# An attention kernel in fp32: another order of eight matmuls in 60 of 1024 steps, and four weight casts a layer given from ScalarE to GpSimd

## The chip, the cores and the metric

The kernel runs on one core of a Trainium2 chip. The metric is the device time of one execution in microseconds (us); lower is better. Times of several executions are given by their median. A profile is one execution recorded instruction by instruction; its times are counted from the first instruction of the program.

Engines are named as in the profile: PE is TensorE (its weight loads are listed apart, as PEld), DVE is VectorE, ACT is ScalarE, POOL is GpSimd, SP is SyncE, which issues most DMAs.

## The reference

Two kinds of layer alternate, twice each, on x of 2048 tokens by 512 values, all in fp32:

```python
x = x + fourier(layernorm(x))     # y = Cr @ (xn @ Dr.T) - Ci @ (xn @ Di.T)
x = x + attention(layernorm(x))   # 32 query heads of 16 values, one shared key and value head
```

The attention is where the change lies:

```python
q = (x @ wq).reshape(B, S, 32, 16).transpose(0, 2, 1, 3)
k, v = x @ wk, x @ wv
p = softmax(einsum("bhqd,bkd->bhqk", q, k) * 16 ** -0.5)
o = einsum("bhqk,bkd->bhqd", p, v).transpose(0, 2, 1, 3).reshape(B, S, 512) @ wo
```

## The kernel before, in words

A "layer" in the code is one Fourier layer (phase a) and the attention layer behind it (phase b); there are two. Most products are made to fp32 accuracy from numbers in two parts: the high part is the number cast to the fast matmul type `F32R`, the low part is the rest, and three matmuls (high x high, high x low, low x high) make one product (`mm3`, lines 87 to 90).

Phase b (line 1278) goes through 16 blocks of 128 queries. A block has 32 steps: two halves of the heads by 16 tiles of 128 keys. A step n belongs to block `i` and has number `s_` in it. In a step TensorE does, in the order written:

- `pv` (line 1103): for the step two before, the product of the probabilities with the values, 8 matmuls of 128 x 512 into a tile of their own, named z (line 1110).
- In steps 1 and 17 of blocks 1 to 15, `o_proj_part` (line 1179): one half of the previous block's output product with `wo`, 6 matmuls (lines 88 to 90) into a PSUM bank of the group y. ScalarE copies the bank out (line 1185), GpSimd adds it to x (line 1188).
- `score` (lines 1087 to 1099), four times: one matmul of 64 rows by 512 columns into a bank of the group x, and on ScalarE the exponential of it into SBUF (line 1098). Even numbers use rows 0 to 63 of the array, odd numbers rows 64 to 127. A score can run beside a matmul in the other half of the rows.
- Maxima for later blocks. The softmax subtracts row maxima, which are found ahead, from the same scores computed once more: `whole(g)` is one matmul of 512 columns in rows half g (line 436) with a reduction on VectorE (line 437). `part(at, 0)` and `part(at, 1)` fill the two halves of one bank with 256 columns each (line 1056), with a copy of one element on VectorE between them (line 1058) and one reduction over both (line 1061).

`share(n)` says how many maxima a step does. It is three in nearly all steps, and then, if `part_next()` finds work, the order is the string in line 1299, `asMssMsb`: a is `part(at, 0)`, b is `part(at, 1)`, M is `whole`, s is `score`; the digits beside the string are the row half, or for s the number of the score. Otherwise the branch at line 1307 goes score by score. The last steps of the last block have no maxima left.

The maxima and the output product share three PSUM banks, the list `o.banks`. Each use takes the first bank of the list and, when its reader is queued, puts it at the end. So in a usual step a takes the bank of the previous step's first M, the first M that of its second M, and the second M that of its b. In a step that begins with a part of the output product, that product takes the first bank, a and the first M the other two, and the second M takes the output product's bank. Every engine works off its queue in the order written, so a matmul that waits for a bank holds up all behind it on TensorE.

The weights `wo` are loaded in four chunks in steps 12 to 15 of block 0 (line 1317) and split into `woh` and `wol` in steps 20, 22, 24 and 26 (lines 1320 to 1322): ScalarE casts the high part (line 79), GpSimd subtracts it (line 80). GpSimd also prepares the maxima for a coming block (lines 589 and 590, called in steps 9 and 25) and issues half of the small DMAs that put them in place (line 601).

Of the kernel before, what the change touches and what calls it, by code (L numbers as in the profile page):

```python
# [22 lines left out]
NT = S // P  # L23
# [25 lines left out]
def fnet_mqa_kernel(ctx: ExitStack, tc: tile.TileContext, x_in, ct, dt_, wq, wkv, wo, out):  # L49
    nc = tc.nc  # L50
# [5 lines left out]
    def f(ap):  # L56
        return ap.bitcast(F32)

    def slot(k, dtype=F32):
        return sb.tile([P, S], dtype, name=f"slot{k}")  # L60

    def half(k, dtype=F32):
        return sb.tile([P, D], dtype, name=f"row{k}")

    def bank(tag):
        return ps.tile([P, 512], F32, name=tag, bufs={"x": 4, "y": 3, "z": 1}[tag])

    def pair():
        return [bank("x") for _ in range(2)]
# [8 lines left out]
    def split_sb(raw, hi, lo, eng=None):  # L78
        nc.scalar.copy(hi, raw)  # L79
        (eng or nc.vector).tensor_sub(lo, raw, f(hi))  # L80
# [116 lines left out]
    def make_layer(L, src, mid, dst, last):  # L197
# [3 lines left out]
        st = {}  # L201
# [818 lines left out]
        def whole(g):  # L1020
            u = next((u for u in ahead if g in u[3]), None)
            if u is None:
                if not todo or todo[0][0] not in o.loaded | {0}:
                    return
                u = (*todo.pop(0), {0, 1})
                ahead.append(u)
            i, pr, kb, gs = u
            max_half(i, pr, g, kb)
            if i + 1 < NT:
                partial(i + 1)  # L1030
            gs.remove(g)
            if not gs:
                ahead.remove(u)
# [4 lines left out]
        def more_max():  # L1038
            whole(side())

        def part_next():
            if parts:
                return *parts.pop(), 1
            for e, (i, pr, kb) in enumerate(todo):
                if i in o.loaded | {0} and kb > 1:
                    parts.append(todo.pop(e))
                    return *parts[0], 0
            return None
# [28 lines left out]
        def share(n):  # L1077
            slack = min([3 * (at - n) - left(j, lim) for j, lim, at in goals if at > n], default=99)
            st["light"] = slack >= SPARE and not st.get("light") and n >= 4
            return 2 if st["light"] else 3  # L1080
# [6 lines left out]
        def score(i, s_, j):  # L1087
            hf, c = divmod(s_, NT)
            jj, g = divmod(j, 2)
            cp = 4 * (2 * hf + jj)  # L1090
            if (i, s_) not in ptiles:
                k = i * NSTEP + s_
                ptiles[i, s_] = slot((6, 7, 2)[k % 3]).rearrange("p (j n) -> p j n", j=4)
            row = o.banks if i == NT - 1 and jj == 1 and not todo + parts + ahead else o.x
            e = row.pop(0)
            nc.tensor.matmul(e, kz[64 * g:64 * g + KR, c * P:(c + 1) * P],  # L1096
                             o.qT[i][64 * g:64 * g + KR, cp:cp + 4, :], start=True, stop=True)
            nc.scalar.activation(ptiles[i, s_][:, j, :], e, AF.Exp, scale=DH ** -0.5)  # L1098
            row.append(e)
# [3 lines left out]
        def pv(i, s_):  # L1103
            hf, c = divmod(s_, NT)
            if c == 0:
                acc[i, hf] = bank("z")
            a = acc[i, hf]
            pt = ptiles.pop((i, s_))
            for j in range(4):
                nc.tensor.matmul(a[32 * j:32 * j + 32, :], v1[:, c, :], pt[:, j, :], start=c == 0, stop=c == NT - 1)  # L1110
            if c == NT - 1:
                oa = half(hf)
                if last and (i, hf) == (NT - 1, 1):
                    ob = half(0)[:, :256]
                    nc.scalar.copy(oa[:, :256], a[:, :256])
                    nc.vector.tensor_copy(ob, a[:, 256:])
                    oa = (oa, ob)
                else:
                    nc.scalar.copy(oa, a)
                acc[i, hf] = oa  # L1120
# [58 lines left out]
        def o_proj_part(i, hf):  # L1179
            po = o.banks.pop(0)  # L1180
            for k in (2 * hf, 2 * hf + 1):
                ks = slice(k * P, (k + 1) * P)
                mm3(po, bt["oh"][:, ks], bt["ol"][:, ks], woh[:, k, :], wol[:, k, :], k == 2 * hf, k == 2 * hf + 1)
            raw = half(4)
            nc.scalar.copy(raw, po)  # L1185
            o.banks.append(po)
            x = bt["x", i]
            nc.gpsimd.tensor_add(x, raw, x)  # L1188
            if hf:
                (nc.sync if last else nc.gpsimd).dma_start(dst[i], x)  # L1190
# [87 lines left out]
        def phase_b(nxt):  # L1278
            nonlocal woh, wol, osp
            o.x = pair() + pair()  # L1280
            o.banks = [bank("y") for _ in range(3)]
            woh = slot(4, F32R).rearrange("p (k e) -> p k e", k=NK)
            wol = slot(5, F32R).rearrange("p (k e) -> p k e", k=NK)
            def wo_load(j):
                st["wo", j] = half(4 + j)
                nc.sync.dma_start(st["wo", j], wo[:, j, :])

            behind = []
            for n in range(NT * NSTEP):
                i, s_ = divmod(n, NSTEP)  # L1290
                if len(behind) == 2:
                    pv(*behind.pop(0))
                behind.append((i, s_))
                if i > 0 and s_ in (1, NT + 1):
                    o_proj_part(i - 1, s_ // NT)
                n_max = share(n) if todo or parts or ahead else 0
                at = part_next() if n_max == 3 else None
                if at:
                    for k, v in zip("asMssMsb", (0, 1, 0, 3, 0, 1, 2, 1)):
                        if k == "s":  # L1300
                            score(i, s_, v)
                        elif k == "M":
                            whole(v)
                        else:
                            part(at, v)
                else:
                    g = side()
                    for j, m in ((g, 0), (1 - g, min(n_max, 2)), (2 + g, 0), (3 - g, n_max - 2)):
                        score(i, s_, j)
                        for _ in range(m):  # L1310
                            more_max()
                if n in (1, 3):
                    q_half_store(12, 2 + n // 2)
                if i == 0 and 17 <= s_ <= 23 and s_ % 2:
                    q_half_store(14, s_ // 2 - 8)
                if 12 <= n < 16:
                    wo_load(n - 12)
                if n == 25:
                    osp = slot(3, F32R).rearrange("p (a h n) -> p a h n", a=2, h=2)
                if i == 0 and s_ in (20, 22, 24, 26):  # L1320
                    j = s_ // 2 - 10
                    split_sb(st["wo", j], woh[:, j, :], wol[:, j, :], nc.gpsimd)
                if i > 0:
                    for fn in out_tasks(i - 1).get(s_, ()):
                        fn()
                for j in range(2, NT):
                    if i == (j // 4 if j < 5 else j - 4 if j < 13 else j - 2):
                        at = {2: 0, 3: 12, 4: 6}.get(j, 0)
                        if s_ == at:
                            qT_load(j)  # L1330
                        if s_ == at + 4:
                            o.loaded.add(j)
                for fn in half_tasks(i).get(s_, ()):
                    fn()
                for at, j, p0, np_ in ((NT - AHEAD, i, HALF, HALF), (NSTEP - AHEAD, i + 1, 0, HALF if i >= NT - 3 else NPAIR)):
                    if j in (0, NT - 2, NT - 1) or j == i + 1 < NT:
                        for e in range(2):
                            if s_ == at - 1 + e:
                                assert done_with(j, p0 + np_ // 2 * (e + 1) - 1)
                                max_neg_a(j, p0, np_, parts=(e,))  # L1340
                        if s_ == at + 1:
                            max_neg_b(np_, nc.gpsimd)
                        if s_ == at + 2:
                            max_rows(j, p0, np_)
            if nxt is not None:
                nxt.a_start()
            for at in behind:
                pv(*at)
            if nxt is not None:
                o.banks = []  # L1350
            return {**out_tasks(NT - 1), 12: [lambda: o_proj(NT - 1)]}
# [18 lines left out]
        woh = wol = osp = None  # L1370
# [48 lines left out]
```

## Time and profile before

| | us |
|---|---|
| median of 3 runs | 3465.91 (3465.49 to 3466.19) |
| profiled execution | 3465.34 |
| its span, from the first to the last instruction | 3463.6 |
| phase b of the first layer, first to last `pv` | 624.7 to 1733.7 |
| phase b of the second layer, first to last `pv` | 2345.0 to 3452.9 |

The two phases b are 1109 + 1108 us of the span, 64%. The mean granted TensorE clock is 0.999 of full speed.

In the lines of the profile, `L1098 ACT ACTIVATE slot<-x` is an instruction of line 1098 on ScalarE that writes a tile named slot and reads one named x; shapes are partitions by elements. A line of the timeline begins with the start and the duration in us; xN says that N instructions in succession are shown as one; a bracket gives the idle time of the engine before it and what ended it. A line of the waits has who waited, for whom, the sum in us, how often, and the longest. A weight load is issued by TensorE just ahead of its matmul; where the matmul has to wait for a bank or for data, it is the load that stands.

### The profile page before, as it was taken

To read this page: it belongs to the slowest core of one execution; us is meant where nothing else is said; L and a number is where in the kernel's file an instruction comes from. 1 tells how busy PE (TensorE), PEld (TensorE's weight loads), DVE (VectorE), ACT (ScalarE), POOL (GpSimd) and SP (SyncE) were. 2 spreads that over 40 slices of the span, in tenths; PEclk is the share of its full clock that TensorE was granted. 3 is DMA by queue.
4 is the path that set the end of the run, shared out by engine and by line. 5 is a ranking of instruction groups with operands and counts; after the bars stand their busy time and mean duration, and the time that the engine had idled before them with its cause. 6 is when DMAs were issued, how large, how long until landed. Compare 5 with 4: busy or idle time off the path is not lost.

```text
span 3463.6 us, 68751 instructions
## 1 busy us (share of the span) xinstructions
PE 3436.3 (99%) x25536; PEld 2020.8 (58%) x25536; DVE 2661.4 (77%) x5774; ACT 2702.7 (78%) x5384; POOL 971.0 (28%) x1500
## 2 busy tenths in 40 slices
PE   8999999999999999999999999999999999999999
PEld 6887979444444444444378989884444444444443
DVE  6264766899999999999432747668999999999992
ACT  4234644899999999999932256549999999999998
POOL 4255453222232222222313454522111111111111
PEclk9999999999999999999999999999999999999999
DMA  5445252311111101111143352523111111011110
GB/s 188 151 154 189 78 170 81 96 51 32 39 41 47 35 27 26 48 35 27 41 140 116 129 169 100 153 71 90 48 39 36 51 35 38 23 39 36 36 26 26
DMA packets 225556, 255.89 MB, mean 74 GB/s; under 512 B 52896, under 2 KB 175040, under 8 KB 218052
## 3 DMA queue, kind: packets, MB, share of 16 engines
q1 hardware_dynamic: 210932, 234.04, 21.9%
q0 software_dynamic: 14144, 17.33, 1.6%
q8 instruction: 201, 3.29, 0.4%
q14 instruction: 135, 1.11, 0.1%
q10 hardware_dynamic: 144, 0.13, 0.0%
HBM read 187.69 MB, written 65.79 MB: 73 GB/s over the span
## 4 chain that ended last, share of the span: by engine, by line
PE 92%; issue 3%; POOL 2%; ACT 1%; DVE 1%; DMA 1%; SPq 0%; DVEq 0%; ACTq 0%; POOLq 0%
PE z L1110 30%; PE x L1096 13%; PE x L879 11%; PE y L1056 10%; PE y L436 8%; PE y L88 3%; PE y L527 3%; PE y L89 3%; PE y L90 3%; PE x L88 2%; PE x L90 2%; PE x L89 2%; PE z L527 1%; PE y L1096 1%; PE z L275 1%
## 5 line engine op out<-in xcount | busy, mean ns | idle before, releaser
L1098 ACT ACTIVATE slot<-x 128x512 f32<-128x512 f32 x3992 | 2055.9, 610 | 29.7 <-PE x L1096 11.1
L437 DVE TENSOR_REDUCE mxp<-y 128x1 f32<-128x512 f32 x1952 | 1261.0, 686 | 61.6 <-PE y L436 7.1
L1110 PE MATMUL z<-slot,v 128*32 128x512 f32 x8192 | 1095.5, 605 | 0.0
L1096 PE MATMUL x<-slot,kz 64*128 64x512 f32 x2968 | 824.2, 429 | 0.3 <-DMA slot<-craw 0.2
L1061 DVE TENSOR_REDUCE mxp<-y 128x2 f32<-128x512 f32 x960 | 655.1, 682 | 0.9 <-PE y L1056 0.9
L1056 PEld LDWEIGHTS y<-kz,slot 64*128 64x128 f32 x1408 | 258.4, 184 | 571.5 <-DVE mxp L437 554.2
L436 PE MATMUL y<-kz,slot 64*128 64x512 f32 x1440 | 572.3, 418 | 0.7 <-DVE mxp L437 0.4
L1096 PEld LDWEIGHTS x<-slot,kz 64*128 64x128 f32 x2968 | 435.2, 184 | 62.2 <-issue 41.0
L1056 PE MATMUL y<-kz,slot 64*128 64x256 f32 x1408 | 465.8, 331 | 0.3
L879 PE MATMUL x<-cl,xnh 64*128 64x512 f32 (+1 forms) x1536 | 357.2, 353 | 0.0
L879 PE MATMUL x<-ch,xnl 64*128 64x512 f32 (+1 forms) x1536 | 345.0, 358 | 3.4 <-ACT xnl L638 3.4
L879 PE MATMUL x<-ch,xnh 64*128 64x512 f32 (+1 forms) x1536 | 346.1, 358 | 0.2
L436 PEld LDWEIGHTS y<-kz,slot 64*128 64x128 f32 x1440 | 263.4, 185 | 83.6 <-DVE y L1058 23.0
L1110 PEld LDWEIGHTS z<-slot,v 128*32 128x32 f32 x8192 | 164.1, 108 | 221.4 <-issue 182.6
L1188 POOL TENSOR_TENSOR row<-row,row 128x512 f32<-128x512 f32 x60 | 77.0, 1283 | 605.6 <-ACT row L1185 605.2
L879 PEld LDWEIGHTS x<-ch,xnh 64*128 64x128 f32 x1536 | 215.3, 184 | 16.5 <-issue 5.1
L879 PEld LDWEIGHTS x<-ch,xnl 64*128 64x128 f32 x1536 | 213.3, 184 | 19.2 <-issue 6.1
L1058 DVE COPY y<-y 1x1 f32<-1x1 f32 x960 | 141.7, 148 | 104.3 <-PE y L1056 95.3
L879 PEld LDWEIGHTS x<-cl,xnh 64*128 64x128 f32 x1536 | 216.8, 185 | 8.0
L79 ACT CAST ch<-craw 128x512 fp32r<-128x512 f32 x176 | 106.6, 625 | 123.1 <-PE x L90 82.6
L527 PE MATMUL y<-kz,slot 64*128 64x512 f32 x488 | 189.1, 397 | 2.8 <-DVE mxe L543 2.2
L1156 POOL TENSOR_TENSOR row<-row,row 128x256 f32<-128x256 f32 x63 | 46.6, 739 | 483.2 <-DMA row<-rd 467.5
(232 smaller groups left out, 5578.9 us busy)
## 6 DMA issues: line engine op xcount, KB each, us to landing
craw<-ct_in SPq DMA_DIRECT2D x112, 512.0 KB
slot<-qd SPq DMA_DIRECT2D x44, 1024.0 KB
qd<-row SPq DMA_DIRECT2D x144, 128.0 KB
od<-row SPq DMA_DIRECT2D x252, 64.0 KB
row<-wqd SPq DMA_DIRECT2D x48, 256.0 KB
row<-x_in SPq DMA_DIRECT2D x32, 256.0 KB
mid<-row POOLq DMA_DIRECT2D x32, 256.0 KB, 2.4
craw<-ct_in SPq DMA_DIRECT2D x32, 256.0 KB
```

What stands on the lines that cost most here:

```text
L88: nc.tensor.matmul(ps_, ah, bh, start=start, stop=False)
L89: nc.tensor.matmul(ps_, ah, bl, start=False, stop=False)
L90: nc.tensor.matmul(ps_, al, bh, start=False, stop=stop)
L436: nc.tensor.matmul(pm, o.qT[i][gs, pr, :], kz[gs, c0:c0 + n], start=True, stop=True)
L437: nc.vector.reduce_max(to, pm, axis=AX.X)
L527: nc.tensor.matmul(pm, o.qT[i][gs, pr, :], k[gs, c0:c0 + 512], start=True, stop=True)
L879: nc.tensor.matmul(z[d], a[gs, s, d * P:(d + 1) * P], b[gs, :], start=first and q < 2 and e == 0, stop=last and q > 1 and e == len(turns) - 1)
L1056: nc.tensor.matmul(pm[:, 256 * g:256 * g + 256], o.qT[i][gs, pr, :], kz[gs, c0:c0 + 256], start=True, stop=True)
L1061: nc.vector.reduce_max(partial(i)[:, pr, :, k], pm.rearrange("p (a n) -> p a n", a=2), axis=AX.X)
L1096: nc.tensor.matmul(e, kz[64 * g:64 * g + KR, c * P:(c + 1) * P], o.qT[i][64 * g:64 * g + KR, cp:cp + 4, :], start=True, stop=True)
L1098: nc.scalar.activation(ptiles[i, s_][:, j, :], e, AF.Exp, scale=DH ** -0.5)
L1110: nc.tensor.matmul(a[32 * j:32 * j + 32, :], v1[:, c, :], pt[:, j, :], start=c == 0, stop=c == NT - 1)
```

## The change

In steps that begin with a part of the output product, and do a part of the maxima (`at`), the order of the eight matmuls becomes `assssMMb`: all four scores first, then the two whole maxima, that of rows half 1 ahead of that of half 0. The halves still alternate from one matmul to the next. All other steps keep their order.

The split of `wo` moves from steps 20, 22, 24, 26 to steps 16, 18, 20, 22 of block 0, and the cast to the high part is an instruction of GpSimd instead of ScalarE. The subtraction stays on GpSimd.

```diff
-                if i > 0 and s_ in (1, NT + 1):
+                out_now = i > 0 and s_ in (1, NT + 1)
+                if out_now:
                     o_proj_part(i - 1, s_ // NT)
                 n_max = share(n) if todo or parts or ahead else 0
                 at = part_next() if n_max == 3 else None
                 if at:
-                    for k, v in zip("asMssMsb", (0, 1, 0, 3, 0, 1, 2, 1)):
+                    order = zip("asMssMsb", (0, 1, 0, 3, 0, 1, 2, 1))
+                    if out_now:
+                        order = zip("assssMMb", (0, 1, 0, 3, 2, 1, 0, 1))
+                    for k, v in order:
...
-                if i == 0 and s_ in (20, 22, 24, 26):
-                    j = s_ // 2 - 10
-                    split_sb(st["wo", j], woh[:, j, :], wol[:, j, :], nc.gpsimd)
+                if i == 0 and s_ in (16, 18, 20, 22):
+                    j = s_ // 2 - 8
+                    nc.gpsimd.tensor_copy(woh[:, j, :], st["wo", j])
+                    nc.gpsimd.tensor_sub(wol[:, j, :], st["wo", j], f(woh[:, j, :]))
```

## Prediction

> **What bounds the kernel now.** I read the page first: busy shares, then the chain of work that ended last.
>
> ```profile
> PE 3436.3 (99%) x25536; PEld 2020.8 (58%) x25536; DVE 2661.4 (77%) x5774; ACT 2702.7 (78%) x5384; POOL 971.0 (28%) x1500
> ...
> PE 92%; issue 3%; POOL 2%; ACT 1%; DVE 1%; DMA 1%; SPq 0%; DVEq 0%; ACTq 0%; POOLq 0%
> PE z L1110 30%; PE x L1096 13%; PE x L879 11%; PE y L1056 10%; PE y L436 8%; PE y L88 3%; PE y L527 3%; PE y L89 3%; PE y L90 3%; PE x L88 2%; PE x L90 2%; PE x L89 2%; PE z L527 1%; PE y L1096 1%; PE z L275 1%
> ```
>
> TensorE is on the chain nearly everywhere, and the attention steps (L1110 values, L1096 scores, L1056 and L436 maxima) are most of it. An average hides which wait ends last, so I went to the busy times of one stretch: 16 steps of block 4 of the second layer, from one step that begins with a part of the output product (I call it an out step) to the next.
>
> ```profile
> 2515.56:2550.42 34.86, 34.86 (x264) 15.60 (x263) 32.30 (x69) 33.72 (x68) 7.77 (x16) 1.00 0.15 39
> ```
>
> The columns are TensorE, weight loads, VectorE, ScalarE, GpSimd, then the clock. Out of 34.86 us TensorE is busy throughout, ScalarE 33.72 and VectorE 32.30. Three engines are nearly full; whoever gains 0.1 us will meet another one. Next the waits, and the timeline of that out step on TensorE (start, duration):
>
> ```profile
> PEld y L436 <- ACT row L1185: 22.2, 58, 0.7
> ```
>
> ```profile
> 2516.56 0.50 PE L88 MATMUL y<-slot,slot 128*128 128x512 f32 x1
> ...
> 2518.15 0.39 PE L1056 MATMUL y<-kz,slot 64*128 64x256 f32 x1
> 2518.16 0.50 PE L1096 MATMUL x<-slot,kz 64*128 64x512 f32 x1
> 2518.38 0.39 PE L436 MATMUL y<-kz,slot 64*128 64x512 f32 x1
> 2518.50 0.50 PE L1096 MATMUL x<-slot,kz 64*128 64x512 f32 x2
> 2518.94 0.49 PE L436 MATMUL y<-kz,slot 64*128 64x512 f32 x1
> 2518.95 0.49 PE L1096 MATMUL x<-slot,kz 64*128 64x512 f32 x1
> 2519.28 0.28 PE L1056 MATMUL y<-kz,slot 64*128 64x256 f32 x1
> 2519.48 1.07 PE L1110 MATMUL z<-slot,v 128*32 128x512 f32 x8
> 2520.48 0.38 PE L1056 MATMUL y<-kz,slot 64*128 64x256 f32 x1
> ...
> 2521.06 0.39 PE L436 MATMUL y<-kz,slot 64*128 64x512 f32 x1
> ```
>
> Six output matmuls, then the eight of the step: a, s, M, s, s, M, s, b. The second M (2518.94) stands for a while: its PSUM bank is the one the output product has just filled, and ScalarE must copy it out first. ScalarE and VectorE at the same place, and the weight loads after it:
>
> ```profile
> 2518.30 0.59 ACT L1185 COPY row<-y 128x512 f32<-128x512 f32 x1 [0.70 <-issue]
> 2518.79 2.07 ACT L1098 ACTIVATE slot<-x 128x512 f32<-128x512 f32 x4
> 2521.02 0.60 ACT L1098 ACTIVATE slot<-x 128x512 f32<-128x512 f32 x1 [0.16 <-PE x L1096]
> ```
>
> ```profile
> 2518.58 0.15 DVE L1058 COPY y<-y 1x1 f32<-1x1 f32 x1 [1.52 <-PE y L1056]
> 2518.81 1.36 DVE L437 TENSOR_REDUCE mxp<-y 128x1 f32<-128x512 f32 x2
> 2520.08 0.68 DVE L1061 TENSOR_REDUCE mxp<-y 128x2 f32<-128x512 f32 x1
> 2520.90 0.15 DVE L1058 COPY y<-y 1x1 f32<-1x1 f32 x1
> 2521.13 1.29 DVE L437 TENSOR_REDUCE mxp<-y 128x1 f32<-128x512 f32 x2
> 2522.33 0.68 DVE L1061 TENSOR_REDUCE mxp<-y 128x2 f32<-128x512 f32 x1
> ```
>
> ```profile
> 2520.83 0.18 PEld L436 LDWEIGHTS y<-kz,slot 64*128 64x128 f32 x1
> ...
> 2521.50 0.16 PEld L1110 LDWEIGHTS z<-slot,v 128*32 128x32 f32 x8 [0.21 <-issue]
> ...
> 2523.07 0.18 PEld L436 LDWEIGHTS y<-kz,slot 64*128 64x128 f32 x1 [0.16 <-DVE y L1058]
> ...
> 2523.61 0.16 PEld L1110 LDWEIGHTS z<-slot,v 128*32 128x32 f32 x8 [0.25 <-issue]
> ...
> 2546.29 0.16 PEld L1110 LDWEIGHTS z<-slot,v 128*32 128x32 f32 x8 [0.23 <-issue]
> 2548.39 0.16 PEld L1110 LDWEIGHTS z<-slot,v 128*32 128x32 f32 x8 [0.25 <-issue]
> 2550.42 0.16 PEld L1110 LDWEIGHTS z<-slot,v 128*32 128x32 f32 x8 [0.23 <-issue]
> ```
>
> The L1110 loads mark the ends of steps: 2519.48, 2521.50, 2523.61. The steps after the out step last 2.02, then 2.11, and go on alternating; near the end of the stretch it is 2.10 and 2.03. The long ones are those in which the second M must wait for VectorE: three banks rotate, and the second M of a step takes the bank that b of the step before used, so it needs that step's last reduction (L1061). At 2522.33 + 0.68 = 2523.01 that ends, and at 2523.07 the load goes. So VectorE's lateness does reach TensorE, in every other step. That decides this case.
>
> **The change, part one: the order.** In an out step the eight become a, s, s, s, s, M, M, b. Both orders alternate between the two halves of the rows. Nothing is added or removed. 58 steps are touched: the wait row counts 58, as there are 30 out steps a layer and the last of each layer has no maxima left.
>
> TensorE in the new step. Up to a (2518.15) nothing moves. The first M is now sixth of eight; in the next step, where nothing waits, the sixth starts 2521.06 - 2520.48 = 0.58 after a, so it runs at 2518.73. The second M now has the awaited bank, so its load still goes at 2518.94. Behind it stand only b, in the other half of the rows, and the values of an earlier step. After a held M, the next matmul on the same rows came 0.34 later (2518.94 to 2519.28), and the values 0.20 after b. With M and b side by side the values come between 2519.28 and 2519.48; I take the middle, 2519.38: a gain of 0.10.
>
> The Trainium skill, "TensorEngine Tiling (Array Packing)", Key Properties, says that changing the tiling mode drains TensorE. By that rule the values, in another mode, cannot load beside M's last columns and the time is 2519.38 or later; without it, it would be 2519.28. The trace agrees so far as the values' loads always come after a gap (0.21 to 0.25).
>
> ScalarE gains nothing. Its four exponentials follow one another from 2518.79, behind the copy, at 0.48 each; the fourth begins at about 2520.23, long after its score (2518.95 + 0.49). Early scores only wait in PSUM.
>
> VectorE loses. Its first reduction follows the first M: in the old order 2518.81, in the new one 2518.73 + 0.39 + 0.04 = 2519.16 (matmul's duration, then the 0.04 from 2518.38 + 0.39 to 2518.81). From the first of two reductions that aren't held up to L1061 it is 2522.33 - 2521.13 = 1.20, so L1061 runs at 2520.36 and ends at 2521.04, instead of 2520.76: 0.28 later.
>
> The next step. a stands 1.00 after the values, at 2520.38. Its second M needs that L1061: load at 2521.04 + 0.06 = 2521.10, where before it went unheld at 2520.83. From a held load to the end of its step it is 2523.61 - 2523.07 = 0.54, so the step ends at 2521.64, not 2521.50: 0.14 later than before, and the gain of 0.10 is gone. In the step after, L1061 of the middle step is no later than before (VectorE had idled before 2520.90 and now does not), the second M isn't held, and the step lasts 2.01 instead of 2.11: 2523.65 against 2523.61, 0.04 late. From there the held and the free steps have changed places, so that the lateness goes 0.14, 0.04, 0.14. Fifteen ordinary steps lie between two out steps; the last of them used to be a free one and is now held. As the alternation has faded by then (2.10 against 2.03), the stretch ends 0.04 + 0.07 = 0.11 late. The next out step starts from there anew. In the first layer's second half-blocks VectorE has statistics to do as well, where held and free steps are less distinct, so I go a little down: 0.10 a step, 58 x 0.10 = 5.8 us lost. Bounds: 0.04 (2.3 us) and 0.14 (8.1 us); beyond them the rivals.
>
> **Part two: the output weights' high part.** Before, ScalarE cast each of four chunks in steps 20 to 26 of block 0 of each layer, and GpSimd subtracted. Now GpSimd does both, four steps earlier. Weight loads at the ends of those steps, one cast, and GpSimd:
>
> ```profile
> 661.78 0.16 PEld L1110 LDWEIGHTS z<-slot,v 128*32 128x32 f32 x8 [0.21 <-issue]
> 663.90 0.16 PEld L1110 LDWEIGHTS z<-slot,v 128*32 128x32 f32 x8 [0.25 <-issue]
> 665.91 0.16 PEld L1110 LDWEIGHTS z<-slot,v 128*32 128x32 f32 x8 [0.20 <-issue]
> 668.33 0.16 PEld L1110 LDWEIGHTS z<-slot,v 128*32 128x32 f32 x8 [0.24 <-issue]
> ```
>
> ```profile
> 665.97 1.28 POOL L80 TENSOR_TENSOR slot<-row,slot 128x512 fp32r<-128x512 f32 x1 [16.54 <-ACT slot L79]
> ```
>
> ```profile
> L227 POOL CAST ch<-craw x80: 601/612/1084, 277.6 to 2284.8; 128x512 fp32r<-128x512 f32 x80
> ```
>
> The step without a cast behind it lasts 663.90 - 661.78 = 2.12, the one after a cast 668.33 - 665.91 = 2.42. So a cast costs 0.30; four in each of two layers, 2.4 us gained. GpSimd pays 0.61 (L227) + 1.28 per chunk, 7.6 us in all, within the 16.54 us that it idles before 665.97. It waits for the chunks' loads only, and no DMA is issued by the moved lines. Queued behind it are the next maxima's rows, which also lose two subtractions that stood ahead of them. If that cover failed, 7.6 us of GpSimd in front of those rows would show as a wait in block 1.
>
> **Sum.** +5.8 - 2.4 = +3.4 us. The profiled run took 3465.34 (span 3463.6 and 1.7 around it), 0.6 under the median, 3465.91. On the median: 3469.3. About 0.2%, 6.9 us, is what a measurement of this kernel can tell from no change; this lies within. The forecast's own range is 58 x 0.04 - 2.4 = 0 to 58 x 0.14 - 2.4 = +5.7 us, 3465.9 to 3471.6.
>
> **Rivals.**
> Faster: VectorE takes up its 0.28 before anyone needs it. Then each out step keeps its 0.10 to 0.20: 58 x 0.10 + 2.4 = 8.2 us to 14.0 us, 3457.7 to 3451.9. For it: VectorE idles 1.52 in the out step. Against it: the second M of the next step needs L1061, and its free load (2520.83) came only 0.07 after the old end (2520.76). It decides if the sixth matmul runs 0.2 earlier than 2518.73. Chance 0.17.
>
> Slower: the 0.28 is never made up, because VectorE sets the pace of all fifteen steps: 58 x 0.28 - 2.4 = +13.8, 3479.7. It decides where VectorE's idle time outside the out step falls under 0.28 a stretch; the stretch above leaves 34.86 - 32.30 - 1.52 = 1.04, which speaks against it, the statistics of the first layer for it. Chance 0.17, with half-way cases from +7.
>
> GpSimd's casts hold VectorE up: 8 x 1.9 = 15 us if it stood all the while, +18 with part one. Two L437 beside a 1.28 us GpSimd addition took 0.69 each (1.36 for the pair, 2518.81), no more than elsewhere. Chance 0.04. The Trainium skill, "SBUF — State Buffer", Who interferes with whom, speaks of a port that GpSimd and VectorE lock against each other, but says that on this chip a reduction never contends; the trace agrees, by that pair.
>
> No effect: held M and L1061 stay as they are, part two is hidden: within 2.4 us. Chance 0.10.
>
> **How the numbers follow.** Forecast 0.52, nearly all of it within 0.2%. Faster is the first rival, 0.17; slower the second and third with a share of the forecast, 0.27; same 0.56. The range must reach into both: 3458 to 3477 leaves out half of the faster rival and the upper part of the slower ones.
>
> **What would show it.** In an out step the second L437's matmul released by the copy, b at its side; the first L437 reduction 0.35 after its old place and L1061 about 0.28; out step 3.8 instead of 3.92, the next 2.25 instead of 2.02; after it even steps long and odd ones short. No ScalarE casts in block 0, steps of 2.12 there. I am wrong if the next step's second M is not held, or if the stretch of 16 steps is under 34.86.

## The result, and the profile after

The kernel after takes 3470.12 us (median of 22 runs) against 3465.09 us before (22 runs): a ratio of 1.0014, 95% interval 1.0008 to 1.0021, or 5.0 us slower (2.8 to 7.3). The forecast was +3.4. The profiled execution took 3469.28 us, 3.9 more than that of before.

First the ends of steps, by the values' weight loads (start, duration), in the same block as before, block 4 of the second layer. 2516.47 is the beginning of the out step.

```profile
2516.47 0.16 PEld L1110 LDWEIGHTS z<-slot,v 128*32 128x32 f32 x8 [0.24 <-issue]
2520.26 0.16 PEld L1110 LDWEIGHTS z<-slot,v 128*32 128x32 f32 x8 [0.24 <-PE y L436]
2522.53 0.16 PEld L1110 LDWEIGHTS z<-slot,v 128*32 128x32 f32 x8 [0.25 <-issue]
2524.55 0.16 PEld L1110 LDWEIGHTS z<-slot,v 128*32 128x32 f32 x8 [0.21 <-issue]
2526.66 0.16 PEld L1110 LDWEIGHTS z<-slot,v 128*32 128x32 f32 x8 [0.25 <-issue]
...
2549.35 0.16 PEld L1110 LDWEIGHTS z<-slot,v 128*32 128x32 f32 x8 [0.22 <-issue]
2551.45 0.16 PEld L1110 LDWEIGHTS z<-slot,v 128*32 128x32 f32 x8 [0.24 <-issue]
```

The out step lasts 3.79 (before 3.92), the next 2.27 (2.02), then 2.02 and 2.11, where it was 2.11 first. The last step of the stretch is a long one, 2.10, where it was 2.03. From 2516.47 to 2551.45 it is 34.98; it was 34.86. So 0.13 is gained in the out step and 0.25 lost right behind it.

TensorE in the out step and the next:

```profile
2519.05 0.38 PE L1056 MATMUL y<-kz,slot 64*128 64x256 f32 x1
2519.06 0.84 PE L1096 MATMUL x<-slot,kz 64*128 64x512 f32 x4
2519.62 0.71 PE L436 MATMUL y<-kz,slot 64*128 64x512 f32 x2
2519.85 0.38 PE L1056 MATMUL y<-kz,slot 64*128 64x256 f32 x1
2520.26 1.06 PE L1110 MATMUL z<-slot,v 128*32 128x512 f32 x8
2521.26 0.38 PE L1056 MATMUL y<-kz,slot 64*128 64x256 f32 x1
...
2521.99 0.49 PE L436 MATMUL y<-kz,slot 64*128 64x512 f32 x1
```

VectorE over the same time:

```profile
2519.47 0.15 DVE L1058 COPY y<-y 1x1 f32<-1x1 f32 x1 [1.56 <-PE y L1056]
2520.05 1.29 DVE L437 TENSOR_REDUCE mxp<-y 128x1 f32<-128x512 f32 x2 [0.42 <-PE y L436]
2521.25 0.68 DVE L1061 TENSOR_REDUCE mxp<-y 128x2 f32<-128x512 f32 x1
2521.85 0.14 DVE L1058 COPY y<-y 1x1 f32<-1x1 f32 x1
```

The bracket of the second row is new: VectorE stands 0.42 until the first maximum, now sixth, has been made. L1061 ends at 2521.25 + 0.68 = 2521.93, and the next step's second maximum (2521.99) goes 0.06 behind it. The weight loads say the same; the first of the two rows is the held maximum of the out step, which waits for ScalarE's copy:

```profile
2519.84 0.18 PEld L436 LDWEIGHTS y<-kz,slot 64*128 64x128 f32 x1 [0.26 <-ACT row L1185]
...
2521.99 0.18 PEld L436 LDWEIGHTS y<-kz,slot 64*128 64x128 f32 x1 [0.30 <-DVE y L1058]
```

Over the whole kernel, who the whole maxima's loads wait for (sum in us, times, longest):

```profile
PEld y L436 <- DVE y L1058: 54.1, 273, 0.3
...
PEld y L436 <- DVE mxp L1061: 15.7, 96, 0.2
PEld y L436 <- ACT row L1185: 15.1, 58, 0.3
```

In the kernel before the rows were 33.7 (201 times), 10.1 (63) and 22.2 (58). The wait for ScalarE's copy has shrunk by 7.1 us; the waits for VectorE have grown by 26.0. The row names L1058, which comes right behind L1061 on VectorE's queue; what the load needs is L1061. In this trace 860 loads of whole maxima begin 0.05 to 0.06 after an L1061 has ended, the free ones among them; to the L1058 beside them they have no fixed distance.

The casts, in block 0 of the first layer:

```profile
654.07 0.61 POOL L1326 CAST slot<-row 128x512 fp32r<-128x512 f32 x1 [4.46 <-DMA row<-wo_in]
654.76 1.29 POOL L1327 TENSOR_TENSOR slot<-row,slot 128x512 fp32r<-128x512 f32 x1
656.00 0.15 POOL L426 MEMSET mxp<- 128x64 f32 x1
...
662.59 1.29 POOL L1327 TENSOR_TENSOR slot<-row,slot 128x512 fp32r<-128x512 f32 x1
```

GpSimd starts as soon as the first chunk has landed and is through with the fourth at 663.88.

### The profile page after: what moved, and what is told of

It is laid out like the page before. It is cut to its first block, busy times and chain, and to the rows that moved or that the text cites. A ratio compares the mean times of both kernels' runs of the same rounds, so it can differ in the third digit from the quotient of the medians.

```text
span 3467.5 us, 68745 instructions
## 1 busy us (share of the span) xinstructions
PE 3440.1 (99%) x25536; PEld 2014.7 (58%) x25536; DVE 2648.9 (76%) x5774; ACT 2696.8 (78%) x5376; POOL 972.6 (28%) x1508
## 4 chain that ended last, share of the span: by engine, by line
PE 91%; issue 3%; POOL 2%; ACT 2%; DVE 1%; DMA 1%; SPq 0%; DVEq 0%; ACTq 0%; POOLq 0%
PE z L1110 29%; PE x L1096 13%; PE x L879 11%; PE y L1056 10%; PE y L436 8%; PE y L88 3%; PE y L527 3%; PE y L89 3%; PE y L90 3%; PE x L88 2%; PE x L90 2%; PE x L89 2%; PE z L527 1%; PE y L1096 1%; DMA craw<-ct_in 1%
## 5 line engine op out<-in xcount | busy, mean ns | idle before, releaser
L437 DVE TENSOR_REDUCE mxp<-y 128x1 f32<-128x512 f32 x1952 | 1256.9, 686 | 78.1 <-PE y L436 31.8
L1096 PE MATMUL x<-slot,kz 64*128 64x512 f32 x2968 | 810.1, 429 | 0.3 <-DMA slot<-craw 0.2
L1061 DVE TENSOR_REDUCE mxp<-y 128x2 f32<-128x512 f32 x960 | 655.1, 682 | 0.9 <-PE y L1056 0.9
L1096 PEld LDWEIGHTS x<-slot,kz 64*128 64x128 f32 x2968 | 427.8, 184 | 59.4 <-issue 41.1
L1058 DVE COPY y<-y 1x1 f32<-1x1 f32 x960 | 141.3, 147 | 103.2 <-PE y L1056 96.4
```

The source lines that it names most:

```text
L437: nc.vector.reduce_max(to, pm, axis=AX.X)
L1061: nc.vector.reduce_max(partial(i)[:, pr, :, k], pm.rearrange("p (a n) -> p a n", a=2), axis=AX.X)
```

## The experiments

Theory V is that of the prediction: the place of the first whole maximum makes VectorE late, L1061 ends late, the next step's second maximum is held, and a loop over two steps hands the lateness on. Rival P: the loss comes from the pair at the end, a held maximum beside b, both loaded late. Rival S: four scores in a row crowd ScalarE. Rival G: the casts on GpSimd cost more than they save. All times below are medians, compared with runs of the kernel before on the same chip.

**The order alone (order_only).** The kernel after, with the old split of the weights put back.

```diff
-                if i == 0 and s_ in (16, 18, 20, 22):
-                    j = s_ // 2 - 8
-                    nc.gpsimd.tensor_copy(woh[:, j, :], st["wo", j])
-                    nc.gpsimd.tensor_sub(wol[:, j, :], st["wo", j], f(woh[:, j, :]))
+                if i == 0 and s_ in (20, 22, 24, 26):
+                    j = s_ // 2 - 10
+                    split_sb(st["wo", j], woh[:, j, :], wol[:, j, :], nc.gpsimd)
```

> The new order alone, with the weight casts left on ScalarE as before. Theory V (VectorE's first reduction comes 0.35 late in the 58 steps, so the next step's second whole maximum is held): out step 3.80, the step after it 2.27, the stretch of 16 steps 0.11 to 0.13 us longer than before; 58 x 0.11 to 0.13 = +6.4 to +7.5 us. If the casts on GpSimd were the loss (rival G), this kernel is as fast as before or faster by up to 6 us.

Measured: 3471.88 against 3465.09, ratio 1.0018 (1.0010 to 1.0027), +6.8 us. The loss is in the order; G falls.

**The casts alone (casts_only).** The kernel before, with that edit made the other way round.

> The old order, with the weight casts on GpSimd in steps 16 to 22. Forecast: the four steps of 2.42 become 2.12, 8 x 0.30 = 2.4 us faster than before. Rival G (GpSimd holds VectorE or the maxima's rows up): slower than before by 2 to 15 us.

Measured: 3463.91 against 3465.09, ratio 0.9994 (0.9985 to 1.0003), -1.2 us: the interval holds both the forecast's -2.4 and no difference, so the total settles nothing beyond that no loss of 2 us or more is there. The steps do: the weight loads at the ends of those steps in this run are

```profile
662.86 0.16 PEld L1110 LDWEIGHTS z<-slot,v 128*32 128x32 f32 x8 [0.20 <-issue]
664.98 0.16 PEld L1110 LDWEIGHTS z<-slot,v 128*32 128x32 f32 x8 [0.25 <-issue]
667.00 0.16 PEld L1110 LDWEIGHTS z<-slot,v 128*32 128x32 f32 x8 [0.20 <-issue]
669.11 0.16 PEld L1110 LDWEIGHTS z<-slot,v 128*32 128x32 f32 x8 [0.25 <-issue]
```

2.12, 2.02, 2.11: the 2.42 are gone. Over 17 steps of block 0 (from step 16 to the next block's first) it is 36.62 before and 35.44 here in the first layer, 36.61 and 35.47 in the second: 2.3 us in both. What hides part of it in the profiled execution stands at the end, under the hardware.

**The first maximum second (max_second).** The kernel after, with one string changed. The held maximum stays seventh, beside b, and the scores stay four in a row.

```diff
-                        order = zip("assssMMb", (0, 1, 0, 3, 2, 1, 0, 1))
+                        order = zip("aMssssMb", (0, 1, 0, 1, 2, 3, 0, 1))
```

> The kernel after, but in the 58 steps the order is a, M (rows half 1), s, s, s, s, M, b: the first whole maximum second of eight, the held one still seventh, beside b. Theory V: the first reduction is not late, L1061 ends within 0.02 of where it did before (0.76 after 2520.00 in the step shown), the gain of 0.10 on TensorE is kept, the next step is 2.02 to 2.05; 58 x -0.10 - 2.4 = 8 us faster than before, ratio 0.9977. Rival P (the loss is that the held maximum stands beside b, both loaded late): as slow as the kernel after, +4 to +5 us. Rival S (scores put together flood ScalarE): as the kernel after.

Measured: 3456.12 against 3465.09, ratio 0.9973 (0.9962 to 0.9983), 9.0 us faster than before and so about 14 faster than the kernel after. VectorE in this kernel's out step, whose a is at 2512.72, and the maxima's loads and ends of steps around it:

```profile
2513.14 0.15 DVE L1058 COPY y<-y 1x1 f32<-1x1 f32 x1 [1.50 <-PE y L1056]
2513.25 1.48 DVE L437 TENSOR_REDUCE mxp<-y 128x1 f32<-128x512 f32 x2
2514.65 0.68 DVE L1061 TENSOR_REDUCE mxp<-y 128x2 f32<-128x512 f32 x1
```

```profile
2510.13 0.16 PEld L1110 LDWEIGHTS z<-slot,v 128*32 128x32 f32 x8 [0.22 <-issue]
...
2513.51 0.18 PEld L436 LDWEIGHTS y<-kz,slot 64*128 64x128 f32 x1 [0.26 <-ACT row L1185]
2513.93 0.16 PEld L1110 LDWEIGHTS z<-slot,v 128*32 128x32 f32 x8 [0.24 <-PE x L1096]
...
2515.39 0.18 PEld L436 LDWEIGHTS y<-kz,slot 64*128 64x128 f32 x1
2515.94 0.16 PEld L1110 LDWEIGHTS z<-slot,v 128*32 128x32 f32 x8 [0.20 <-issue]
```

The out step is 3.80, as in the kernel after: the held pair (2513.51, waiting for the same copy) costs no more. But the first reduction follows the copy at once, L1061 ends 2515.33 - 2512.72 = 2.61 after a (kernel after: 2.88; before: 2.61), the next load (2515.39), 0.06 behind it, comes in time, without a wait in its row, and the next step is 2.01. P and S fall: scores and held pair are as in the kernel after, and the loss is not there.

**The first maximum fourth (max_fourth).** Again one string.

```diff
-                        order = zip("assssMMb", (0, 1, 0, 3, 2, 1, 0, 1))
+                        order = zip("assMssMb", (0, 1, 0, 1, 2, 3, 0, 1))
```

> The kernel after, but in the 58 steps the order is a, s, s, M (rows half 1), s, s, M, b: the first whole maximum fourth. Theory V: its reduction starts about 0.11 later than in the old order and 0.24 earlier than in the new one; but the second reduction waits for the held maximum at the same place as in the old order (2519.48 in the step shown), so L1061 ends at most 0.05 late and the next step is 2.02 to 2.07; 58 x -0.06 to -0.10 - 2.4: 6 to 8 us faster than before. If lateness counts in proportion to the first reduction's place, with no slack in between, it would be a third of the way from max_second to the kernel after: 4 to 5 us faster than before.

Measured: 3456.95 against 3464.83, ratio 0.9977 (0.9968 to 0.9986), 7.9 us faster, within V's 6 to 8. The interval (4.9 to 11.1 us) hardly shuts out the 4 to 5 of a loss in proportion to the place, but the steps do: out step 3.80, next step 2.04 on average, and a stretch lasts 34.80, the same as in max_second (the kernel after: 35.03), where a third of the way would be 34.88. What counts is not the place itself but when the last reduction ends, and that hardly moves as long as the second reduction is ready by the time the held maximum is made.

This run also shows that the sums of the wait rows are no prices. The whole maxima's loads wait 9.1 + 5.9 = 15.0 us for VectorE here and 38.6 + 11.1 = 49.7 in max_second, which is no slower. The ordinary steps mostly alternate between 2.04 and 2.09 here and between 2.01 and 2.12 there; two of them together last 4.13 in both.

**VectorE late, the order untouched (vector_late).** The kernel before, with one reduction more on VectorE in the 58 steps; its result is not used.

```diff
                         else:
+                            if v == 1 and i > 0 and s_ in (1, NT + 1):
+                                nc.vector.reduce_max(sb.tile([P, 1], F32, name="late"), f(kz[:, :208]), axis=AX.X)
                             part(at, v)
```

> The kernel before, old order and old casts, with one more VectorE reduction (128 x 208 of an SBUF tile that is constant here, about 0.28 us) ahead of the last reduction of the 58 steps; it reads no PSUM and nothing uses its result. Theory V: the out step stays at 3.92, L1061 of that step 0.28 later, the next step 2.16 instead of 2.02, held and free steps change places, the stretch 0.11 longer: +6 us, although TensorE's order is the old one. Rivals P and S: VectorE's idle time takes it up, 0 us, within 0.05%.

Measured: 3471.39 against 3465.09, ratio 1.0018 (1.0009 to 1.0027), +6.3 us, from 58 instructions. VectorE, and the maxima's loads and ends of steps:

```profile
2521.38 1.35 DVE L437 TENSOR_REDUCE mxp<-y 128x1 f32<-128x512 f32 x2
2522.65 0.36 DVE L1306 TENSOR_REDUCE late<-kz 128x1 f32<-128x208 f32 x1
2522.92 0.69 DVE L1061 TENSOR_REDUCE mxp<-y 128x2 f32<-128x512 f32 x1
```

```profile
2522.05 0.16 PEld L1110 LDWEIGHTS z<-slot,v 128*32 128x32 f32 x8 [0.25 <-PE x L1096]
...
2523.66 0.18 PEld L436 LDWEIGHTS y<-kz,slot 64*128 64x128 f32 x1 [0.21 <-DVE y L1058]
2524.21 0.16 PEld L1110 LDWEIGHTS z<-slot,v 128*32 128x32 f32 x8 [0.25 <-issue]
...
2526.22 0.16 PEld L1110 LDWEIGHTS z<-slot,v 128*32 128x32 f32 x8 [0.20 <-issue]
```

L1061 comes 0.27 later (2522.92 instead of 2522.65), ends at 2523.61, and the load goes at 2523.66. The next step is 2.16, the one after it 2.01: held and free steps have changed places, with TensorE's old order. This reproduces the kernel after's trouble without its order.

**Both together (second_late).** The kernel max_second with the same reduction.

```diff
                         else:
+                            if v == 1 and out_now:
+                                nc.vector.reduce_max(sb.tile([P, 1], F32, name="late"), f(kz[:, :208]), axis=AX.X)
                             part(at, v)
```

> The kernel max_second (first whole maximum second of eight) with the same additional VectorE reduction of about 0.28 us in the 58 steps as in vector_late. Theory V: L1061 is as late against the output product as in the kernel after, so nearly all that max_second gained over it goes: out step 3.80, next step 2.25 to 2.28, held and free steps change places, stretch 35.0; 4 to 6 us slower than before. Rivals P and S (where scores and maxima stand decides, not VectorE): within 2 us of max_second, 7 to 9 us faster than before.

Measured: 3470.06 against 3464.83, ratio 1.0014 (1.0005 to 1.0023), +5.2 us: the whole gain of 9.0 is gone, and the time is that of the kernel after (3470.12). Next step 2.27, as there.

**The same order in every step (second_all).** The order of max_second in all steps with a part and two whole maxima.

```diff
-                    order = zip("asMssMsb", (0, 1, 0, 3, 0, 1, 2, 1))
-                    if out_now:
-                        order = zip("assssMMb", (0, 1, 0, 3, 2, 1, 0, 1))
+                    order = zip("aMssssMb", (0, 1, 0, 1, 2, 3, 0, 1))
```

> The order a, M, s, s, s, s, M, b in every step with a part and two whole maxima, not in the 58 alone. Theory V read on: the maximum that needs the previous step's last bank now stands seventh, not sixth, 0.2 later in the step, and the first reduction starts earlier, so no ordinary step has a held maximum; the alternation of 2.01 and 2.12 becomes 2.01 to 2.03 throughout. About 900 such steps, 0.04 to 0.055 each: 36 to 50 us faster than max_second, 45 to 58 us faster than before, ratio 0.983 to 0.987. Rival (another wait takes its place, as VectorE and ScalarE are busy 32.3 and 33.7 of 34.9 us already): steps stay at 2.05 to 2.07 on average, within 5 us of max_second.

Measured: 3540.69 against 3464.83, ratio 1.0221 (1.0207 to 1.0235), 76 us slower. My reading-on was wrong, and the rival too put the price at nothing. No ordinary maximum is held by L1061 any more, but another row of its waits has grown (before: 16.6 us, 36 times):

```profile
PEld x L1096 <- ACT slot L1098: 142.9, 519, 0.8
```

473 of the 519 are the fourth score of a step, which uses the bank that the previous step's fourth exponential frees. In the row of the busy times for one long step,

```profile
2675.44:2677.66 2.22, 2.22 (x18) 0.87 (x17) 2.13 (x5) 2.20 (x6) 0.00 (x0) 1.00 0.00 0
```

ScalarE (fifth number) is busy 2.20 of 2.22 us; that alone tells little, as it is busy 2.11 of 2.11 in the kernel before's step from 2521.50 to 2523.61. By the waits S is true of ordinary steps, where scores in a row run into ScalarE, and not of the out steps, where six output matmuls give ScalarE time to empty the banks. No run moves the scores of the ordinary steps without their maxima, so for these steps the cause is read from the waits and not tested.

**b sixth, the second maximum last, in the ordinary steps** (`"asMssbsM"`), with the out steps of max_second (b_sixth) and with those of the kernel after (b_sixth_new).

```diff
-                    order = zip("asMssMsb", (0, 1, 0, 3, 0, 1, 2, 1))
+                    order = zip("asMssbsM", (0, 1, 0, 3, 0, 1, 2, 1))
```

> max_second, and in the ordinary steps the order a, s, M, s, s, b, s, M: the second part of the split bank sixth, the second whole maximum last. Scores stay in their places, so ScalarE is not bunched as in second_all. The bank that the previous step's last reduction frees (now the second whole maximum's) is then asked for a whole step later; no maximum of an ordinary step waits for the reduction just before it. Theory V with its loop of two steps (previous last reduction, held maximum, values, next step's maxima): without the loop the alternation of 2.01 and 2.12 goes, steps 2.01 to 2.03; about 900 x 0.04 = 36 us faster than max_second, 45 us faster than before, ratio 0.987. If the alternation has another cause: within 5 us of max_second.

> The same order in the ordinary steps, with the order of the kernel after (a, s, s, s, s, M, M, b) in the 58 steps. Theory V: VectorE is as late after the 58 steps as in the kernel after, but the only maximum that meets it is last in the next step and no loop hands it on: 58 x 0 to 0.13 = 0 to 8 us slower than b_sixth, instead of the 14 us between the kernel after and max_second. If the place of the scores in the 58 steps decided, the 14 us stay.

Measured: 3548.81 against 3465.86 for the first, ratio 1.0240 (1.0226 to 1.0254); 3557.49, ratio 1.0266 (1.0252 to 1.0280), for the second. They are 83 and 92 us slower, so the forecast of the total failed by far, and its rival (within 5 us of max_second) as well. The ordinary steps are 2.17, nearly all alike, and long for a reason that the forecast had left out; the waits of the first of the two have

```profile
PEld y L1056 <- DVE y L1058: 200.3, 900, 0.4
```

b fills the second half of a's bank and needs VectorE's copy of one element (L1058) out of its first half. As the sixth matmul it asks too early and its load stands 0.22 on average, 900 times. Each step is then a chain of its own: in one step of b_sixth a comes 1.00 after the values (2667.67), b 0.63 after a (2668.30), the next values 0.54 after b (2668.84), 2.17 in all. With this chain in charge the alternation would be gone whatever had made it, so the two runs are no test of the loop.

Between the two kernels lie 8.7 us, just above V's 0 to 8 and well under the 14 of the rival: the order of the kernel after costs 0.17 in the next step (2.33 against 2.17), and nothing is added or made up after it. It is VectorE's lateness again, by a way that was not forecast: L1061 ends late (2681.41 in block 4 of the second layer), the L1058 behind it on VectorE's queue is late too, and b goes 0.79 after a instead of 0.63.

## Why the prediction was right

**The gain on TensorE.** Put at 0.10; 0.13 in the step shown (3.92 to 3.79). The values follow the held load by 0.42 (2519.84 to 2520.26); I had taken 0.44. By the drain rule of the Trainium skill ("TensorEngine Tiling (Array Packing)", Key Properties) it was to be 0.44 or more, without a drain 0.34; the trace has 0.42 to 0.43 in all 58 steps, nearer to the rule but under the bound worked out from it, and again the load comes after a gap, 0.24.

**VectorE's lateness.** Put at 0.28; L1061 ends 2.88 after a instead of 2.61, 0.27 later. Shown as the cause, not only argued: with the lateness and without the order the loss is there (+6.3), with the order's crowded scores and held pair and without the lateness it is not (-9.0), and putting the lateness back brings it back (+5.2). The last two kernels have the casts on GpSimd, so 2.3 us of their gain is not the order's; between the two, which have it alike, lie 14 us.

**The next step and the loop.** Next step 2.26 by the prediction's ends (2521.64 - 2519.38), 2.27 measured. Held and free steps change places as forecast.

**The price of a stretch.** This term was sized a little low. Put at 0.10, it averages 0.116 over the 56 stretches of blocks 1 to 14: first halves 34.88 to 35.01 and 34.89 to 35.00 in the two layers, second halves 35.02 to 35.11 and 34.88 to 35.01. The first layer's second halves are indeed the cheapest (0.09). 56 x 0.116 = 6.5, and 0.05 more in the last blocks: 6.6, where the order alone measured 6.8 and the prediction said 5.8.

**What the loop sets.** The prediction's rows also give the length of its loop, which it did not add up: 1.00 from the values to a, 0.65 to the first reduction (2520.48 to 2521.13), 1.20 to L1061, 0.68 for it, 0.06 to the held load, 0.54 to the end of that step, 4.13 for two steps. Two ordinary steps together do last 4.13 to 4.14 on average in every run that keeps their order (4.15 to 4.16 in the first layer's second halves), whichever of the two is the long one. So the last fourteen steps of a stretch cost nearly the same before and after (0.02 less after), and what a stretch loses is lost in its first two: 0.12 gained in the out step, 0.26 lost in the next. No run shortens a link of the loop, so that it sets the pace of the ordinary steps is worked out here and not tested.

**The casts.** Put at -2.4; 2.3 in the steps. GpSimd took 1.9 us a chunk, as put, and ended at 663.88 after a pause between the first two chunks; six L437 between 658 and 664 took 680 to 692 ns, so VectorE wasn't held up. What I had missed: on GpSimd's queue the first cast also came ahead of a memset and two copies for the second next block's maxima (L426, 648.95 before, 656.00 now). No wait in the trace comes of it.

**The sum** by steps is 6.6 - 2.3 = +4.3, by the two experiments +6.8 - 1.2 = +5.6, measured +5.0. The prediction took 0.2%, 6.9 us, for the least that can be told from no change; with 22 runs of each kernel 5.0 us can be told.

The faster rival failed at the condition named for it: the sixth matmul ran 0.57 after a, not 0.2 earlier. (The range's lower end, 3458, left out all of that rival's 3451.9 to 3457.7, and not half, as the prediction has it.) The slower one, 0.28 lost in every stretch, did not come either, as it left out what the out step gains: 0.26 lost in the next step less 0.12 gained is 0.14, and 0.12 of that is left at the end of the stretch.

## What to carry to other kernels

When three engines are each over 90% busy, filling a hole on one of them is not yet a gain: ask which engine begins later because of it, and who asks for its result in the next round. In a rotation of buffers, look for the loop (here reduction, held maximum, values, next maxima) and keep its first link early; in the out steps the scores could then stand together (max_second) or in pairs (max_fourth) and the gain stayed. An order that pays after a long pause need not pay in the ordinary round: the order of max_second, faster in the 58 steps, made the kernel 85 us slower than max_second when nearly all steps had it.

## What the runs showed of the hardware

TensorE's granted clock (the third number from the end) can drop for some microseconds as the attention phase begins. Busy times of two stretches there, of the run with the casts alone, and below of the kernel before:

```profile
621.00:623.30 2.30, 1.99 (x10) 0.87 (x10) 2.30 (x6) 1.40 (x4) 2.13 (x6) 1.00 0.78 264
623.30:626.80 3.50, 3.46 (x16) 1.24 (x16) 2.53 (x5) 2.67 (x6) 0.48 (x4) 0.51 0.83 258
```

```profile
621.00:623.30 2.30, 1.98 (x10) 1.00 (x10) 2.30 (x6) 1.39 (x4) 2.08 (x4) 1.00 0.90 264
623.30:626.80 3.50, 3.39 (x28) 1.73 (x30) 3.28 (x8) 3.45 (x8) 0.71 (x5) 1.00 0.84 268
```

With the same ten matmuls in the 2.3 us ahead, the clock is 0.51 in the one and 1.00 in the other, and 16 matmuls are done instead of 28. A mean of 0.51 over 3.50 us is 3.4 us at half the clock. The first step there lasts 2.87 instead of 2.00. The second layer has such a step too, 2.96 in the run with the casts alone, 2.69 in the profile of before and 2.01 in that of after. These differences, up to 0.9 us a layer here and 1.2 in the profile of max_fourth (a first step of 3.25), come and go between profiles of kernels that do the same work up to there, and are no part of the change; with them, the run with the casts alone shows 2.3 - 0.9 - 0.3 = 1.1 us less than before instead of 2.3 (its profiled execution took 3464.37, 1.0 less). The Trainium skill, "TensorE: Matmul & The Clock Gate", What's actually happening, tells of a gate that halves the clock after an idle window of about 3.4 us and opens again after a busy one as long, the windows running free of the kernel. The half clock and its length agree; an idle window does not show, as TensorE is busy 1.99 of the 2.30 us ahead. No run here tested the cause.
